# Windowed attention and a two-layer MLP on one core: chunk 0 in two halves, signs by the leaky function, words in pairs, two convolutions shared with VectorE

## The chip, the cores and the metric

One core of a Trainium2 chip runs the program. The time is device microseconds (us) from launch to end of one execution; the figure of a kernel is the median of its runs.

## What is computed

```python
# x (4, 4096, 192) and weight_gen (4, 4096, 8, 7) float32; w_in (192, 2048) and w_out (2048, 192) float64
w = softmax(weight_gen, axis=-1)                 # 7 taps for each of 8 heads of each token
out[b, s] = sum over k of w[b, s, :, k] * x[b, s - 6 + k]     # a causal convolution, 24 channels a head
h = out.reshape(16384, 192) @ w_in               # 16384 x 2048
g = maximum(0.01 * h, h)
y = g @ w_out                                    # 16384 x 192, float32
```

The two matrices come as 64-bit numbers, so a kernel reads them as pairs of 32-bit words and makes float32 values of them on the chip.

## The kernel before

**Tiling.** Partition p holds 128 consecutive tokens, its rows. A chunk is 4 rows of all partitions, that is 512 tokens; there are 32 chunks, and two chunks share one piece of loaded rows and softmax weights. The 2048 hidden units are 16 blocks of 128, taken two at a time in 8 steps per chunk (`NQ`).

**Work of a chunk.** GpSimd (POOL in the profile) convolves it (`conv_ops`: seven products of 768 elements per partition, six additions). The result is brought into the transposed form `xx`. TensorE multiplies with `w_in` (`mm1`), ScalarE (ACT) applies the leaky maximum, ScalarE and VectorE (DVE) split the result into a rounded part `gh` and a rest `gl`, and TensorE multiplies both with `w_out` into `po`. Operands of chunks 1 to 31 are split so, into two parts of a type that TensorE takes in one pass; a float32 product takes it four.

**Preparing the matrices.** Each of the 16 keys (8 steps, in and out) goes through stages: `read_words` (`r`, two ScalarE instructions, into `rnd` and `mag`), `widen` (`w` or `W`: VectorE shifts `mag` left by three, L121, then takes the sign in with a second instruction, L124), the rounding (`W`: VectorE L130; `o`: GpSimd L135), and, for later chunks, `upper_half` (`u` ScalarE L153, `U` VectorE L151) and `lower_half` (`L` VectorE, `l` GpSimd, L157). `spares` is a bank of PSUM that VectorE uses as scratch.

**The start.** Chunk 0 runs with the unsplit float32 values as they become ready (`mm1` with `value(...)`, `mm2_whole`, L437), so that the split parts are only wanted from chunk 1 on. Its convolution is divided by heads between VectorE (`d`, 20 of 32 row-heads, its products and its scratch in PSUM) and GpSimd (`g`). Chunk 1 is convolved by GpSimd alone (`p`), and so is chunk 2 (`q`, `feed`). `heat` issues 12 matmuls of zeros ahead of the first transposes. Chunks 0 and 1 are transposed by TensorE (`transposes`, L290; rows L299 and L300 move the result), later ones by VectorE and DMA.

**What sets the order.** Each engine runs its instructions in the order of the program. The string `START` lists the work of the start letter by letter: `s` is the next step of TensorE, the other letters are the stages above. Behind the string, `step` lays out the steady state.

## Time and profile before

| | |
|---|---|
| median of 3 runs | 1160.31 us (1159.36 to 1160.99) |
| the profiled execution's own time | 1161.17 us |
| its span, first to last instruction | 1159.4 us |
| TensorE busy | 1142.1 us (99%) |
| GpSimd, ScalarE, VectorE busy | 782.2, 645.1 and 514.2 us |
| mean granted TensorE clock | 0.998 |
| HBM read and written | 31.98 and 12.58 MB |

The span is what the rows of the trace add up to; the execution's own time is 1.8 us longer and holds what lies around it. The chain of waits is followed back from the last instruction and tells on which engine the end hangs at each moment. Busy shares are averages over the whole span: VectorE with 44% over all is busy 36.5 of the 40 us from 10 to 50, in the start.

### The profile page before, as it was taken

The page shows a single profiled execution, that of the slowest core. Times are in us where ns is not written, and L with a number is a line of the kernel's source. Part 1 is how long each engine was busy: PE and PEld are TensorE (multiplying, and loading weights), DVE is VectorE, ACT ScalarE, POOL GpSimd, SP SyncE. Part 2 cuts the span into 40 slices and gives each one's busy share as a digit, 9 for nine tenths or more (in the row PEclk, how much of TensorE's full clock was granted, in tenths as well). Part 3 has the DMA queues.
Part 4 walks back from the last instruction along what each step waited for, and adds up shares of the span by engine and source line. Part 5 has one row for each costly group of instructions (what it writes and reads, how often), then busy time and mean ns, then how long its engine had stood idle before and what let it go on. Part 6 is the DMA issues. An engine that isn't in the chain of part 4 may idle for free.

```text
span 1159.4 us, 30227 instructions
## 1 busy us (share of the span) xinstructions
PE 1142.1 (99%) x12660; PEld 1023.7 (88%) x12660; DVE 514.2 (44%) x829; ACT 645.1 (56%) x1173; POOL 782.2 (67%) x495
## 2 busy tenths in 40 slices
PE   5999999999999999999999999999999999999998
PEld 3689999999999999999999999999999999999997
DVE  7954343444334444344443444443444443444432
ACT  4656555565555555555555455555555555555554
POOL 7888687666687666787666786666786667876300
PEclk9999999999999999999999999999999999999999
DMA  8502422323233231322313224232322314222210
GB/s 230 156 18 73 119 55 70 115 53 99 67 91 92 56 104 49 111 70 70 108 48 109 56 69 120 51 103 60 110 72 60 108 43 121 60 69 56 52 46 15
DMA packets 43093, 93.70 MB, mean 81 GB/s; under 512 B 9679, under 2 KB 25167, under 8 KB 41166
## 3 DMA queue, kind: packets, MB, share of 16 engines
q1 hardware_dynamic: 42814, 91.59, 28.9%
q8 instruction: 99, 1.62, 0.6%
q14 instruction: 36, 0.29, 0.1%
q10 hardware_dynamic: 144, 0.20, 0.0%
HBM read 31.98 MB, written 12.58 MB: 38 GB/s over the span
## 4 chain that ended last, share of the span: by engine, by line
PE 98%; DVE 1%; DMA 0%; ACT 0%; issue 0%; SPq 0%; DVEq 0%
PE po L398 48%; PE hp L350 47%; PE po L437 2%; DMA xt<-in_x_dram 0%; DVE spares L251 0%; DVE acc L256 0%; PE ta L290 0%; DVE twice L266 0%; ACT hp L356 0%; DVE gl L373 0%; DVE xx L300 0%; ACT gh L372 0%; ACT xx L299 0%; DVE ot L474 0%; DVE bits L124 0%
## 5 line engine op out<-in xcount | busy, mean ns | idle before, releaser
L373 DVE TENSOR_TENSOR gl<-hp,gh 128x512 fp32r<-128x512 f32 x496 | 343.3, 692 | 558.1 <-ACT gh L372 557.5
L398 PE MATMUL po<-wo,gh 64*128 64x384 f32 x3968 | 581.3, 353 | 0.0
L356 ACT ACTIVATE hp<-hp 128x512 f32<-128x512 f32 x496 | 292.3, 589 | 434.3 <-PE hp L350 434.2
L398 PE MATMUL po<-wo,gl 64*128 64x192 f32 x3968 | 497.8, 248 | 0.3 <-DVE gl L373 0.3
L350 PE MATMUL hp<-xx,wi_h 64*128 64x512 f32 x2976 | 472.8, 395 | 0.1
L398 PEld LDWEIGHTS po<-wo,gl 64*128 64x128 f32 x3968 | 378.4, 187 | 11.1 <-DVE gl L373 0.5
L398 PEld LDWEIGHTS po<-wo,gh 64*128 64x128 f32 x3968 | 372.7, 184 | 11.8
L256 POOL TENSOR_TENSOR acc<-acc,tmp 128x768 f32<-128x768 f32 (+1 forms) x190 | 346.1, 1822 | 14.6
L372 ACT CAST gh<-hp 128x512 fp32r<-128x512 f32 x496 | 291.8, 588 | 38.6 <-PE po L398 24.8
L350 PEld LDWEIGHTS hp<-xx,wi_h 64*128 64x128 f32 x2976 | 260.2, 184 | 46.3 <-DVE xx L300 0.4
L251 POOL TENSOR_TENSOR tmp<-xt,wt 128x768 f32<-128x768 f32 (+1 forms) x192 | 291.8, 1520 | 12.4
L350 PE MATMUL hp<-xx,wi_l 64*128 64x512 f32 x1488 | 294.3, 391 | 0.0
L350 PEld LDWEIGHTS hp<-xx,wi_l 64*128 64x128 f32 x1488 | 140.1, 184 | 33.0
L310 POOL TENSOR_TENSOR split<-acc,split 128x768 fp32r<-128x768 f32 x30 | 55.3, 1843 | 167.4 <-ACT split L306 167.4
L474 DVE TENSOR_TENSOR ot<-po,ot 128x384 f32<-128x384 f32 x62 | 34.6, 558 | 69.6 <-ACT ot L473 69.2
L211 POOL TENSOR_TENSOR wt<-wt,mx 128x448 f32<-128x448 f32 (+1 forms) x16 | 15.2, 950 | 71.5 <-DVE mx L208 71.4
L319 DVE STREAM_TRANSPOSE sq<-split 128x384 f32<-128x384 f32 x120 | 58.5, 544 | 0.0
L251 POOL TENSOR_TENSOR acc<-xt,wt 128x768 f32<-128x768 f32 (+1 forms) x32 | 48.9, 1527 | 0.2
L225 POOL TENSOR_TENSOR wt<-wt,sm 128x448 f32<-128x448 f32 (+2 forms) x17 | 15.5, 915 | 37.6 <-DVE sm L222 29.5
L473 ACT COPY ot<-po 128x384 f32<-128x384 f32 x62 | 29.7, 479 | 6.4 <-PE po L398 3.6
L306 ACT CAST split<-acc 128x768 fp32r<-128x768 f32 x30 | 25.0, 833 | 0.0
L437 PEld LDWEIGHTS po<-bits,g 128*128 128x128 f32 x128 | 20.6, 190 | 4.9 <-DVE spares L121 1.5
(56 smaller groups left out, 219.6 us busy)
## 6 DMA issues: line engine op xcount, KB each, us to landing
xx<-sq SPq DMA_DIRECT2D x480, 96.0 KB, 2.2
xt<-in_x_dram SPq DMA_DIRECT2D x14, 1344.0 KB, 5.8
out_dram<-ot SPq DMA_DIRECT2D x63, 192.0 KB, 1.9
...
```

The lines of the kernel that those rows point to most:

```text
L251: ins = eng.tensor_tensor(out=out, in0=xv[:, s, :], in1=wk, op=ALU.mult).ins
L256: eng.tensor_tensor(out=acc[:, s, :], in0=acc[:, s, :], in1=out, op=ALU.add)
L310: eng.tensor_tensor(out=l, in0=att.pop(c), in1=h.bitcast(F32), op=ALU.subtract)
L319: nc.vector.transpose(out=sq[c][:, v, i], in_=src[:, v])
L350: nc.tensor.matmul(out=hp[2 * q + u], lhsT=w[s], rhs=r[s], start=(m == 0), stop=(m == len(passes) - 1),)
L356: return nc.scalar.activation(out=hp[n], in_=hp[n], func=AF.Prelu, alpha=0.01).ins
L372: nc.scalar.copy(out=h, in_=t)
L373: nc.vector.tensor_tensor(out=l, in0=t, in1=h.bitcast(F32), op=ALU.subtract)
L398: ins = nc.tensor.matmul(out=po[j // HALF][:, j % HALF, 0:d], lhsT=g[n][s, j * P:(j + 1) * P], rhs=wo[s, f, 0:d], start=(f == 0 and i < HA ...
L437: nc.tensor.matmul(out=po0[:, j // 2, j % 2 * D:(j % 2 + 1) * D], lhsT=g_h[n][:, j * P:(j + 1) * P], rhs=value((n // 2, OUT))[:, n % 2], s ...
L473: nc.scalar.copy(out=ot, in_=po[k][:, :, D:2 * D])
L474: nc.vector.tensor_tensor(out=ot, in0=po[k][:, :, 0:D], in1=ot, op=ALU.add)
```

## The change

Six things are changed, all in the first 90 us of the program.

- Chunk 0 is computed in two halves of two rows (`first_step`, 16 steps of 256 tokens). The first half runs in float32 as before. The second half takes the split parts of `w_in` and of its tokens (`split_passes`), so `wi_h` and `wi_l` are wanted eight steps earlier. Both halves still multiply with the unsplit `w_out` values. Only the first two rows are convolved ahead of the first transposes (`d` and `g`, 10 of 16 row-heads on VectorE); the other two are GpSimd's alone (`e`).
- ScalarE's leaky function with a slope of -2^32 makes `mag`, so that its bits carry the sign; VectorE's second instruction of `widen` (L124) is gone.
- Words come in pairs of blocks: runs of 2048 and 3072 bytes instead of 1024 and 1536, in half as many issues. Hidden units are dealt to the blocks in another order, the same for both matrices.
- VectorE convolves one of four rows of chunk 1 (`P`) and two of four rows of chunk 2 (`Q`), with its scratch `tmpd` in SBUF.
- `heat` is three portions of 5 instead of one of 12.
- The order `START` is new. More of the casts (`U`) are VectorE's: 10 instead of 1.

```diff
 START = (
-    "ASdrrggggdgddggdggadgdrwgZdgddddgdobTWrppppppppWpkKWrspWrrWsrrsWWMrpspWr"
-    "WruspLrUuWrLWuEsDrwrLsouWWuLLuqqWlqquqsqLLqquqqqIusLLusuqsLuLquCVyuqqLsL"
-    "YLusXqqqXqqsqqXqlXqsqs"
+    "ArSdZggdggddddggggdgZgddZgaddgdgrjdbTreesUjjUKrjerrwsjLpurseoeleeerrjjre"
+    "seursWuejrersepjrjjrpUpjlLrsstppUUUjplLPpPsulsUpPpppPPsssspMLkLPEUPPPPDl"
+    "PuPqPlQlUqsQsQqQqqIqqUsqqQQqsqlQlQqqQQQqqsQQCVsuyYslqXqqXqqqqsqXXqslqqqs"
+    "q"
 )


...
+    def load_words(j, kind):
+
         if kind == IN:
-            w = raw.tile([P, NB, P, 2], U32, tag="wi", name="wi_raw", bufs=3)
+            w = raw.tile([P, NB, 2 * P, 2], U32, tag="wi", name="wi_raw", bufs=2)
             for u, r in enumerate(HALVES):
-                f = 2 * q + u
-                eng.dma_start(out=w[r], in_=w_in_words[:, :, f * P:(f + 1) * P, :])
+                f = u * DFF // 2 + 2 * j * P
+                nc.sync.dma_start(out=w[r], in_=w_in_words[:, :, f:f + 2 * P, :])
+            w = w.rearrange("p b (m v) w -> p v b m w", v=2)
         else:
-            w = raw.tile([P, 2, D, 2], U32, tag="wo", name="wo_raw")
-            eng.dma_start(out=w, in_=w_out_words[:, 2 * q:2 * q + 2, :, :])
-        words[key] = w
+            w = xtp.tile([P, 2, 2, D, 2], U32, tag="xx", name="wo_raw", bufs=2)
+            nc.sync.dma_start(out=w, in_=w_out_words[:, :, j])
+            w = w.rearrange("p u v d w -> p v u d w")
+        for v in range(2):
+            words[2 * j + v, kind] = w[:, v]

     NW = NB * P
     vals = {}

...
-        nc.scalar.activation(out=rnd, in_=w[:, :, 0], func=AF.Copy, scale=2.0 ** -29)
-        nc.scalar.activation(out=mag, in_=w[:, :, 1].bitcast(F32), func=AF.Copy, scale=REBIAS)
+        w = words.pop(key)
+        rnd = raw.tile([P, NW], U32, tag="rnd", name="rnd", bufs=4)
+        mag = raw.tile([P, NW], F32, tag="mag", name="mag", bufs=4)
+        a = NB if key[1] == IN else 2
+        flat = [t.rearrange("p (a b) -> p a b", a=a) for t in (rnd, mag)]
+        nc.scalar.activation(out=flat[0], in_=w[..., 0], func=AF.Copy, scale=2.0 ** -29)
+        nc.scalar.activation(
+            out=flat[1], in_=w[..., 1].bitcast(F32), func=AF.Prelu, scale=REBIAS, alpha=SIGN
+        )
         vals[key] = rnd, mag.bitcast(U32)

...
+    def widen(keys, add=False):
+
+        slots = [spare().bitcast(U32) if add else None for _ in keys]
+        for key, t in zip(keys, slots):
+            rnd, mag = vals[key]
+            bits = raw.tile([P, NW], U32, tag="bits", name="bits", bufs=NV)
+            vals[key] = bits, rnd
+            if t is None:
+                t = bits
+            nc.vector.tensor_scalar(
+                out=t, in0=mag, scalar1=3, scalar2=None, op0=ALU.logical_shift_left
+            )
+        for key, t in zip(keys, slots):
+            if add:
+                bits, rnd = vals[key]
+                nc.vector.tensor_tensor(out=bits, in0=t, in1=rnd, op=ALU.add)
+                vals[key] = bits.bitcast(F32)

...
+    def conv_ops(c, eng, tag, r0=0, n=J, inner=None, outer=None, tmp=None, w=None):

         if c not in att:
             att[c] = conv.tile([P, J, D], F32, tag="acc", name="acc", bufs=2)
-        acc = att[c].rearrange("p r (h g) -> p (r h) g", g=G)
-        q, i0 = c // 2, c % 2 * J
+        acc = att[c][:, r0:r0 + n, :].rearrange("p r (h g) -> p (r h) g", g=G)
...
             s = inner if k else outer
-            n = s.stop - s.start
-            xv = xt[q][:, i0 + k:i0 + k + J, :].rearrange("p r (h g) -> p (r h) g", g=G)
-            wk = w[:, s, k:k + 1].to_broadcast([P, n, G])
+            m = s.stop - s.start
+            xv = xt[q][:, i0 + k:i0 + k + n, :].rearrange("p r (h g) -> p (r h) g", g=G)
+            wk = w[:, s, k:k + 1].to_broadcast([P, m, G])
             if k == K - 1:
                 out = acc[:, s, :]
             else:
-                t = conv.tile([P, J * D], F32, tag=tag, name=tag) if tmp is None else tmp
-                out = t[:, 0:n * G].rearrange("p (h g) -> p h g", g=G)
+                if tmp is None:
+                    t = conv.tile([P, n * D], F32, tag=tag, name=tag)
+                else:
+                    t = tmp[:, k % 2 * TOK:(k % 2 + 1) * TOK]
...
+    def transposes_first(h):
+
+        if h:
+            new_xx(0)
+        for b in range(NB):
+            t = ps_h.tile([P, TOK], F32, tag="h", name="ta")
+            for j in range(HALF):
+                v = twice[0][:, (h * HALF + j) * NB + b].rearrange("p u d -> p (u d)")
+                nc.tensor.transpose(out=t[:, j * P:(j + 1) * P], in_=v, identity=ident)
+            if h == 0:
+                if b == 1:
+                    nc.vector.tensor_copy(xx0[:, b], t[:, 0:HT])
+                else:
+                    nc.scalar.copy(out=xx0[:, b], in_=t[:, 0:HT])
+                continue
+            t = t[:, 0:HT].rearrange("p (j t) -> p j t", j=HALF)
+            hi, lo = (xx[0][:, 0:HALF, v, b, :] for v in range(2))
+            nc.scalar.copy(out=hi, in_=t)
+            nc.vector.tensor_tensor(out=lo, in0=t, in1=hi.bitcast(F32), op=ALU.subtract)
...
+    def split_passes(i, tokens):
+
+        assert (i, IN) in halved
         passes = []
         for b in range(NB):
-            h, l = xx[c][:, :, 0, b, :], xx[c][:, :, 1, b, :]
-            w_h, w_l = wi_h[:, i, b, :], wi_l[:, i, b, :]
-            if c == 0:
-                passes.append((value((i, IN))[:, b], h))
-            else:
-                passes += [(w_h, h), (w_h, l), (w_l, h)]
+            (h, l), w_h, w_l = tokens(b), wi_h[:, i, b, :], wi_l[:, i, b, :]
+            passes += [(w_h, h), (w_h, l), (w_l, h)]
+        return passes
+
...
+    def first_step(m):
+
+        h, i = divmod(m, NQ)
+        if h == 0:
+            passes = [(value((i, IN))[:, b], xx0[:, b]) for b in range(NB)]
+        else:
+            passes = split_passes(
+                i, lambda b: [xx[0][:, 0:HALF, v, b, :] for v in range(2)]
+            )
+        hs = [ps_h.tile([P, TOK], F32, tag="h", name="hp")[:, 0:HT] for u in range(2)]
+        products(passes, hs)
+        for u in range(2):
+            g = gp.tile([P, TOK], F32, tag="gh", name="g")[:, 0:HT]
+            nc.scalar.activation(out=g, in_=hs[u], func=AF.Prelu, alpha=0.01)
+            g_h[2 * m + u] = g
+        if m >= 2:
+            mm2_whole(m - 2)

...
+    def mm2_whole(m):
+
+        h, i = divmod(m, NQ)
+        for u in range(2):
+            for j in range(HALF):
                 nc.tensor.matmul(
-                    out=po0[:, j // 2, j % 2 * D:(j % 2 + 1) * D],
-                    lhsT=g_h[n][:, j * P:(j + 1) * P], rhs=value((n // 2, OUT))[:, n % 2],
-                    start=(n == 0 and j % 2 == 0), stop=(n == NF - 1 and j % 2 == 1),
+                    out=po0[:, h, j * D:(j + 1) * D],
+                    lhsT=g_h[2 * m + u][:, j * P:(j + 1) * P], rhs=value((i, OUT))[:, u],
+                    start=(i == 0 and u == 0 and j == 0),
+                    stop=(i == NQ - 1 and u == 1 and j == HALF - 1),
                     skip_group_check=True,
...
-    stages = dict(r=read_words, w=widen, o=round_up, u=upper_half, l=lower_half)
-
-    stages["W"] = lambda key: widen(key, True)
+    stages = dict(r=read_words, o=round_up, u=upper_half, l=lower_half)
...
-        w0 = po0[:, 0, 0:J * HK].rearrange("p (h k) -> p h k", k=K)
+        w0 = po0[:, 0, 0:HALF * HK].rearrange("p (h k) -> p h k", k=K)
         away = spares.rearrange("p a b -> p (a b)")
+        parts = slice(0, G0), slice(0, (HALF - C0) * H)
+        rest = slice(G0, HALF * H), slice((HALF - C0) * H, HALF * H)
         conv0 = dict(
-            d=conv_ops(0, nc.vector, None, slice(0, G0), slice(0, (J - C0) * H), away, w0),
-            g=conv_ops(0, nc.gpsimd, "tmp", slice(G0, J * H), slice((J - C0) * H, J * H)),
-            p=conv_ops(1, nc.gpsimd, "tmp"),
+            d=conv_ops(0, nc.vector, None, 0, HALF, *parts, away, w0),
+            g=conv_ops(0, nc.gpsimd, "tmp", 0, HALF, *rest),
+            e=conv_ops(0, nc.gpsimd, "tmp", HALF, HALF),
+            P=conv_ops(1, nc.vector, "tmpd", 0, C1),
+            p=conv_ops(1, nc.gpsimd, "tmp", C1, J - C1),
+            Q=conv_ops(2, nc.vector, "tmpd", 0, C2),
         )
+
...
             elif what == "A":
                 tell(softmax_max(0, FIRST))
-                load_words(order[0])
+                load_words(0, IN)
                 load_weights(0, SECOND)
-                load_words(order[1])
-                load_rows(0, ((PAD + J, PAD + R),))
-                load_words(order[2])
-                load_words(order[3])
+                load_rows(0, ((PAD + HALF, PAD + R),))
+                load_words(1, IN)
+                load_words(0, OUT)
                 softmax_sub(0, nc.vector, FIRST)
                 softmax_exp(0, FIRST)
             elif what == "S":
```

TensorE at its start. The names: `ta<-ident,twice` are the transposes, `hp` the first product, `po` the second. Before:

```order
L290 MATMUL ta<-ident,twice 128x128 x12
L350 MATMUL hp<-xx,bits 128x512 x18
L437 MATMUL po_105<-bits,g 128x192 x8
L350 MATMUL hp<-xx,bits 128x512 x6
L437 MATMUL po_105<-bits,g 128x192 x8
```

Now:

```order
L330 MATMUL ta<-ident,twice 128x128 x6
L394 MATMUL hp<-xx0_89,bits 128x256 x18
L509 MATMUL po_106<-bits,g 128x192 x4
L394 MATMUL hp<-xx0_89,bits 128x256 x6
L509 MATMUL po_106<-bits,g 128x192 x4
```

Half as many transposes and second products, and first products of half as many columns, stand in each step; there are twice as many steps.

VectorE between the last words and the transposed chunk 1 (`xx<-ta,xx` is its lower half, which TensorE waits for). Before:

```order
L130 ISA bits<-spares,rnd 128x768
L157 TENSOR_TENSOR wo<-bits,wo 128x2x192
L157 TENSOR_TENSOR wi_l<-bits,wi_h 128x384
L121 TENSOR_SCALAR spares<-mag 128x384
L124 SCALAR_TENSOR_TENSOR spares<-mag,spares 128x384
L130 ISA bits<-spares,rnd 128x768
L157 TENSOR_TENSOR wi_l<-bits,wi_h 128x384
L157 TENSOR_TENSOR wo<-bits,wo 128x2x192
L300 TENSOR_TENSOR xx<-ta,xx 128x4x128 x3
```

Now, from the lower half of chunk 0's second rows to the last words and the first products of chunk 1:

```order
L340 TENSOR_TENSOR xx<-ta,xx 128x2x128 x3
L172 CAST wi_h<-bits 128x384 x2
L172 CAST wo<-bits 128x2x192
L143 TENSOR_SCALAR spares<-mag 128x384
L149 ISA bits<-spares,rnd 128x768
L178 TENSOR_TENSOR wi_l<-bits,wi_h 128x384
L283 TENSOR_TENSOR acc<-xt,wt 128x192
L283 TENSOR_TENSOR tmpd<-xt,wt 128x192
L172 CAST wo<-bits 128x2x192
L280 TENSOR_TENSOR acc<-acc,tmpd 128x192
```

and from the end of VectorE's row of chunk 1 to the lower half of the transposed chunk 1:

```order
L283 TENSOR_TENSOR tmpd<-xt,wt 128x192
L306 TENSOR_TENSOR twice<-acc,tmpd 128x3x64
L283 TENSOR_TENSOR acc<-xt,wt 128x384
L172 CAST wo<-bits 128x2x192
L283 TENSOR_TENSOR tmpd<-xt,wt 128x384
L280 TENSOR_TENSOR acc<-acc,tmpd 128x384
L283 TENSOR_TENSOR tmpd<-xt,wt 128x384
L355 TENSOR_TENSOR xx<-ta,xx 128x4x128 x3
```

Three casts stand ahead of the last words, and five instructions of chunk 2 and of the casts stand between `twice`, which the transposes of chunk 1 read, and the lower half of their result.

## Rows read from the trace of the kernel before

**Rows 1.** The page, part 4: the chain that ended last, share by engine.
```profile
PE 98%; DVE 1%; DMA 0%; ACT 0%; issue 0%; SPq 0%; DVEq 0%
```

**Rows 2.** The chain of waits in order of time: start us, us, what.
```profile
17.19 2.80 PE ta L290 x12
...
28.26 2.80 PE po L437 x16
31.06 2.78 PE hp L350 x12
...
60.76 2.35 PE hp L350 x16
63.11 5.40 PE po L437 x32
68.51 4.38 PE hp L350 x36
72.89 2.27 PE po L398 x32
```

**Rows 3.** Timeline, TensorE, second set of transposes: start us, us, engine, line, operation.
```profile
58.76 1.47 PE L290 MATMUL ta<-ident,twice 128*128 128x128 f32 x12
```

**Rows 4.** Windows of 1 us, TensorE: busy, granted clock (PEclk), DMA share, GB/s.
```profile
16.00:17.00 1.00, 0.00 (x0) 1.00 1.12 300
...
18.00:19.00 1.00, 1.00 (x7) 0.50 0.15 28
```

**Rows 5.** Timeline, VectorE and GpSimd, convolution of chunk 0.
```profile
5.62 0.65 DVE L251 TENSOR_TENSOR acc<-xt,po 128x480 f32<-128x480 f32 x1
...
6.19 0.69 POOL L251 TENSOR_TENSOR acc<-xt,wt 128x288 f32<-128x288 f32 x1
...
7.61 0.79 POOL L256 TENSOR_TENSOR acc<-acc,tmp 128x288 f32<-128x288 f32 x1
...
13.30 0.58 POOL L211 TENSOR_TENSOR wt<-wt,mx 128x224 f32<-128x224 f32 x1
...
15.50 0.52 POOL L251 TENSOR_TENSOR tmp<-xt,wt 128x192 f32<-128x192 f32 x1
...
16.10 1.14 POOL L266 TENSOR_TENSOR twice<-acc,tmp 128x192 f32<-128x192 f32 x2
```

**Rows 6.** Timeline, VectorE, casts and differences with both inputs in SBUF.
```profile
37.80 1.96 DVE L151 CAST wi_h<-bits 128x384 fp32r<-128x384 f32 x1
...
52.27 0.55 DVE L157 TENSOR_TENSOR wi_l<-bits,wi_h 128x384 fp32r<-128x384 f32 x1
...
54.49 1.37 DVE L157 TENSOR_TENSOR wi_l<-bits,wi_h 128x384 fp32r<-128x384 f32 x1
55.78 1.90 DVE L157 TENSOR_TENSOR wo<-bits,wo 128x384 fp32r<-128x384 f32 x1
```

**Rows 7.** Timeline, GpSimd, at the same times.
```profile
37.43 2.11 POOL L256 TENSOR_TENSOR acc<-acc,tmp 128x768 f32<-128x768 f32 x1
...
52.56 1.11 POOL L157 TENSOR_TENSOR wo<-bits,wo 128x384 fp32r<-128x384 f32 x1 [0.64 <-ACT wo L153]
53.63 1.81 POOL L256 TENSOR_TENSOR acc<-acc,tmp 128x768 f32<-128x768 f32 x1
55.52 1.74 POOL L251 TENSOR_TENSOR tmp<-xt,wt 128x768 f32<-128x768 f32 x1
57.34 2.02 POOL L256 TENSOR_TENSOR acc<-acc,tmp 128x768 f32<-128x768 f32 x1
59.44 1.54 POOL L251 TENSOR_TENSOR tmp<-xt,wt 128x768 f32<-128x768 f32 x1
```

**Rows 8.** Groups of instructions from 0 to 60 us: busy us, mean ns, idle before.
```profile
L124 DVE SCALAR_TENSOR_TENSOR spares<-mag,spares 128x384 uint32<-128x384 uint32 x14 | 7.9, 561 | 0.5
L130 DVE CUSTOM_DVE_ANT_0 bits<-spares,rnd 128x768 uint16<-128x768 uint16 x14 | 7.8, 557 | 0.8
...
L112 ACT ACTIVATE rnd<-wi_raw 128x384 uint32<-128x384 uint32 x8 | 4.5, 560 | 8.3 <-DMA wi_raw<-in_moe_w_in_dram 8.0 <-ACT mag L113 0.2
```

191 lines of the change are left out of this document (97 added, 94 removed).

## The prediction

> **What bounds the kernel now.** The first view to read is the chain that ended last: TensorE holds 98% of it [rows 1]. A change can therefore gain only where TensorE gets less to do, starts earlier, or stands still less. The chain in order of time says where that could be [rows 2]. TensorE's first useful work, the transposes of chunk 0, begins at 17.19 us; from then to 63.11 it goes through chunk 0 and the first product of chunk 1, each step of chunk 0 costing 2.78 for the first product (12 float32 passes) and 2.80 for the second. At 63.11 two leftover second products of chunk 0 follow (5.40), and at 68.51 the split steady state begins. The change leaves what comes from there to 1159.4 as it is, so I compare the moment that answers to 68.51.
>
> Two further views belong to it. The windows show that TensorE's granted clock was at its lower level (0.50, 1.2 GHz) while the first transposes ran, after a window in which TensorE did nothing [rows 4]; those 12 took 2.80, the next 12 took 1.47 at full clock [rows 3]. And the timelines of VectorE and GpSimd side by side show what no busy share shows: a VectorE instruction with both inputs in SBUF does not run beside a GpSimd instruction. The one at 52.27 started while GpSimd was idle and took 0.55. The one at 54.49 took 1.37: GpSimd's instruction ended at 53.63 + 1.81 = 55.44, VectorE's 0.42 later. The next started at 55.78 and took 1.90, again 0.42 behind GpSimd's end at 57.26; and a cast, started at 37.80, ended 0.22 behind GpSimd's [rows 6, 7]. These waits cost nothing before, since few of them stood in front of anything that TensorE wanted.
>
> **The change part by part.** All is counted against the profiled span, 1159.4; its execution took 1161.17, 0.86 above the median of 1160.31, and I add the difference to the median.
>
> *Earlier start.* Half the rows are convolved before the first transposes. GpSimd's share is the later one. Its costs per element follow from the rows: products 0.52 at 192 and 0.69 at 288 elements, additions 0.79 at 288 and 1.81 at 768, the softmax subtraction 0.58 at 224 [rows 5, 7]. That gives 0.44 for a product and 0.48 for an addition of 144, 0.77 for the subtraction of 336, 1.00 for the last addition of 384. Six products of 144, one of 192, five additions, the subtraction and the last addition are 2.64 + 0.52 + 2.40 + 0.77 + 1.00 = 7.33; some 11 gaps of 0.08 (0.79 + 0.08 is the usual distance) make 8.2. It begins about 0.3 earlier than 6.19, as the first softmax has half the elements. 5.9 + 8.2 = 14.1: **3.1 earlier**. VectorE's share (0.65 at 480 elements, so about 0.41 at 240) is done a microsecond before that.
>
> *TensorE's work.* First half of chunk 0: eight first products on half the columns, between 1.39 (half of 2.78) and 1.51 (if 0.07 per pair of passes is fixed), I take 1.45; six second products on half the rows, 1.40 each: 11.6 + 8.4 = 20.0. Second half: the first product is 18 single-pass matmuls in 9 pairs. Pairs of 512 columns cost 4.38 / 18 = 0.243, pairs of 288 on average 2.27 / 16 = 0.142 [rows 2], so 256 columns cost 0.13 and the step 1.16; with eight second products 9.3 + 11.2 = 20.5. The last two second products, 2.8, come behind chunk 1's first product. Transposes: 0.73 + 0.73 + 1.47; chunk 1's first product 2.19. Sum 48.4. Three times TensorE waits for the transposed tile to be moved: 4.35 - 1.47 - 2.19 = 0.7 for chunk 1 (58.76 to 63.11), some 0.4 for each half-size one: 1.5. Before, the stretch from 17.19 to 68.51 was 51.3, now 49.9: **1.4 less**, of which 1.3 is the clock. If the clock is low under the first six transposes they cost up to 0.7 more; portions of `heat` now come up to their start, so I take none. Without further waits the kernel gains 4.5: 1155.8.
>
> *Signs.* Fourteen of the sixteen removed L124 took 7.9 us of VectorE [rows 8]. VectorE was not on the path; ScalarE's instruction for `mag` keeps its size. Nothing by itself. *Words in pairs.* ScalarE waited 8.0 us for words of `w_in` [rows 8], TensorE never did. The bytes are the same, the runs twice as long: between 0 and, if two large buffers come free later than three small ones, the same 0 as long as ScalarE keeps ahead (a rival below).
>
> *VectorE's share of chunks 1 and 2, and nine more casts.* This is the part that adds waits. VectorE's own work is small: 192 elements with both inputs in SBUF cost 0.35 alone (0.55 at 384). But `tmpd`, `xt`, `wt` and the casts' sides are all SBUF, and GpSimd is convolving at the same time, with instructions of 576 elements, 1.20 and 1.40 long by the prices above. By rows 6 and 7 each such VectorE instruction ends 0.2 to 0.4 after the end of the GpSimd instruction that it meets, and the next one meets the next: one VectorE instruction per GpSimd instruction, 1.3 to 1.5 us instead of 0.35. I walk through VectorE's order behind the lower half of chunk 0's second rows, which is done near 38.0 (14.1 + 0.7 + 0.4 + 20.0 = 35.2, with about 0.8 of waits for the first words 36.0; transposes and the moving add 2.0).
>
> - Three casts stand ahead of the last words. At 1.35 each they end at 42.1; shift and rounding (0.56 + 0.56) give the words at 43.2. TensorE wants them after 36.0 + 1.1 + 1.16 + 1.40 + 1.16 = 40.9. **Wait 2.3** (0 if the casts meet an idle GpSimd: 38.0 + 1.05 + 1.1 = 40.2).
> - Seven more at 1.3 take VectorE to 52.2, where GpSimd's part of chunk 1 is done and it waits for VectorE's maximum for the next softmax. Then VectorE is nearly alone: maximum 0.6, two differences 1.7 (one meets the subtraction), six short products, additions and a cast 2.0, the sums 1.35, one more 0.35, together 6.0, to 58.2; the last two of chunk 1 meet GpSimd again, 1.0 each, to 60.2; ScalarE's copy of 768 elements, some 0.8, gives 61.0. TensorE wants chunk 1 at 43.2 + 1.40 + 6 x 2.56 = 60.0. **Wait 1.0.**
> - The transposes end at 62.5. Their lower half stands behind five instructions of chunk 2 and casts, 1.1 each: 60.2 + 5.5 + 0.7 = 66.4, where 62.8 would do. **Wait 3.6.** This is the largest.
> - Behind it VectorE has nine more instructions of chunk 2, 0.55 alone and up to 1.8 each, among the differences `gl` of chunk 1, which TensorE waits for. **Wait 1.0 to 1.7**, I take 1.5.
>
> The sum is 2.3 + 1.0 + 3.6 + 1.5 = 8.4 of new waits against 4.5 gained: 3.9 longer, or 1160.3 + 3.9 = **1164.2**. The weakest term is the meeting of the two engines: VectorE's instructions are short, so 2% on GpSimd's durations moves each wait by up to one GpSimd instruction.
>
> A rule goes further here. The rows show a GpSimd instruction behind such a meeting lengthened by 0.20 to 0.29 (1.74 against 1.54, 2.02 against 1.81, 2.11 against 1.81) [rows 7]. The Trainium skill, SBUF — State Buffer, section Who interferes with whom, says that whoever has the shared port pair holds it for the whole instruction and the other fully blocks; by that rule GpSimd would lose VectorE's 0.55. The waiting agrees with the trace; the length does not, as VectorE's start-up falls into its wait, and I price it by the rows.
>
> **The rivals.**
>
> *VectorE's waits are hidden (faster).* The place is the same: from 38 to 66 us. If VectorE's instructions mostly fall into GpSimd's gaps, or the last words and `xx` come in time, TensorE goes through as in the sum without waits: 1155.8. For it: GpSimd is idle in places, and VectorE's own work from 38 to the lower half of chunk 1 is only some 14 us of 22. It decides when fewer than about six of the 26 such instructions in that stretch wait. Against it: all three that met GpSimd in rows 6 waited to its end.
>
> *Half of it hidden (no change).* The casts and `twice` come in time, the five of chunk 2 do not: -4.5 + 3.6 + 1.0 = about 1160.4. The point is whether GpSimd's durations of 576 elements are a few per cent shorter than I interpolate.
>
> *GpSimd loses the whole instruction.* If its instructions lengthen by 0.41, VectorE's reading time, and not by 0.20, the ten waits in the first two places grow by 0.2 each: 2 us, 1166.2. The sentence of the skill above would bring this about.
>
> *ScalarE paces the first half.* Each step now has four reads of words of 0.56 and two leaky functions of at most 0.56 in 2.85 us of TensorE: 3.36 if nothing overlaps [rows 8]. Up to 0.5 a step, 4 us: 1168.
>
> **How the numbers follow.** Forecast 1164.2 with chance 0.5, its own range 1162.7 to 1167.5; GpSimd loses more 0.07; ScalarE paces 0.05; half hidden 0.18; all hidden 0.2. Faster by over 0.2% (below 1158.0; that is about the least that a measurement of this kernel can tell from no change) is nine tenths of the hidden case with a fifth of the middle one: 0.22. Within 0.2%, up to 1162.6, is what is left of these two and the low end of the forecast: 0.19. Slower: 0.59. The range reaches up to 1168, where ScalarE paces, and down to 1156.5, which takes in about half of the hidden case.
>
> **What would show it.** In the changed profile the first transposes should start near 14 at full clock; the steps of the first half cost 2.85, those of the second 2.56. The casts L172 and the products L283 of VectorE with `tmpd` should have means of 1 us and more, ending 0.2 to 0.4 behind GpSimd's; the chain should name VectorE's `bits`, `twice` and `xx` between 38 and 66, some 7 us together. If L283 on VectorE has a mean near 0.4 instead, the sum falls back to 1156. If the first half's steps are 3.3 apart with ScalarE in the chain, the fourth rival holds. If the steady state behind it is not as long as before, my comparison at 68.51 was too short.

## The result and the profile after

The changed kernel takes 1172.9 us (median of 4 runs, 1172.68 to 1173.32), the kernel before 1160.3: a ratio of 1.011, interval 1.0092 to 1.0127. It is 12.6 us slower where 3.9 were predicted. Its profiled execution took 1172.68 with a span of 1170.6, 11.2 longer than that of before.

Before itself gives two times: of 19 executions in one batch, 11 took 1159.35 to 1159.79 at a mean granted clock of 0.999 to 1.000 and 8 took 1160.70 to 1161.01 at 0.998, and the profile behind [rows 2, 4] is of the second kind (1161.17).

Below, "before" and "after" are the two kernels. The page of after, chain by engine, answers to [rows 1]: TensorE's share of the chain fell from 98% to 91%.

```profile
PE 91%; DVE 4%; ACT 2%; issue 1%; SPq 1%; DMA 1%; ACTq 0%
```

The chain of after in order of time (start us, us, what) answers to [rows 2].

```profile
13.72 1.47 PE ta L330 x6
15.19 2.67 PE hp L394 x12
...
20.18 0.78 ACT mag L129
21.74 0.66 ACT g L428 x2
22.80 0.79 ACT rnd L128
...
41.42 1.77 DVE wi_h L172 x2
43.20 1.07 DVE wo L172
...
67.76 0.69 DVE xx L355
68.49 3.91 PE hp L394 x17
72.40 2.80 PE po L509 x16
75.20 2.34 PE hp L394 x18
...
84.25 1.80 DVE tmpd L283
86.07 1.78 DVE acc L280
87.85 1.20 DVE gl L446 x2
...
97.20 0.59 SPq L384
97.83 0.59 SPq L384
...
107.15 2.54 PE po L469 x32
```

From 18 to 36 the chain runs mostly through ScalarE, from there to 68 through VectorE, from 80 to 90 again, and from 97 to 107 through SP's queue, where the 16 transfers of chunk 2 are issued one by one (0.59 each), late. The point that answers to 68.51 of before is 75.20, 6.7 later; another 4.5 are lost behind it. What TensorE waited for behind 60 (us in total, times, longest):

```profile
PE hp L394 <- DVE xx L355: 3.0, 1, 3.0
PE po L469 <- DVE gl L446: 2.1, 1, 2.1
PE po L469 <- SPq L483: 0.6, 1, 0.6
```

Behind two of these waits the granted clock (PEclk, the third number from the right) goes to its lower level, 0.50, as it did under the first transposes of before [rows 4]. Windows of after:

```profile
68.00:69.00 1.00, 0.51 (x4) 0.42 (x6) 1.00 (x3) 0.00 (x0) 0.92 (x2) 0.81 0.00 0
70.00:71.00 1.00, 1.00 (x8) 0.81 (x6) 0.00 (x0) 0.00 (x0) 0.92 (x2) 0.50 0.00 0
...
91.00:92.00 1.00, 1.00 (x8) 0.80 (x6) 0.00 (x0) 0.97 (x3) 0.89 (x1) 0.50 0.00 0
```

The product at 68.49 took 3.91 (17 of its 18 records) where the same product of before took 2.35 at full clock (16 of 18) [rows 2].

The transfers are late because chunk 2 is. GpSimd's first product of it, before and after:

```profile
48.89 1.54 POOL L251 TENSOR_TENSOR acc<-xt,wt 128x768 f32<-128x768 f32 x1
```

```profile
61.68 0.99 POOL L283 TENSOR_TENSOR acc<-xt,wt 128x384 f32<-128x384 f32 x1
```

The last additions of chunk 2 after, GpSimd's for its two rows and VectorE's for the other two, and then ScalarE's rounding of the whole chunk in before (that of after, at 90.20, is shown further down):

```profile
82.59 1.21 POOL L292 TENSOR_TENSOR acc<-acc,tmp 128x384 f32<-128x384 f32 x1
89.55 0.56 DVE L292 TENSOR_TENSOR acc<-acc,tmpd 128x384 f32<-128x384 f32 x1
```

```profile
76.50 0.84 ACT L306 CAST split<-acc 128x768 fp32r<-128x768 f32 x1
```

GpSimd is done at 83.80, VectorE at 90.11: in the changed kernel the rounding waits for VectorE's rows.

### The profile page after: what moved, and what is told of

Its sections match the earlier page's. It is cut to its first block, busy times and chain, and to the rows that moved or that the text cites. A ratio compares the mean times of both kernels' runs of the same rounds, so it can differ in the third digit from the quotient of the medians.

```text
span 1170.6 us, 30566 instructions
## 1 busy us (share of the span) xinstructions
PE 1149.8 (98%) x12807; PEld 1035.5 (88%) x12807; DVE 525.5 (45%) x842; ACT 648.2 (55%) x1183; POOL 788.4 (67%) x515
## 4 chain that ended last, share of the span: by engine, by line
PE 91%; DVE 4%; ACT 2%; issue 1%; SPq 1%; DMA 1%; ACTq 0%
PE po L469 47%; PE hp L394 44%; DVE tmpd L283 1%; SPq L384 1%; DVE acc L280 1%; DMA wt<-in_weight_gen_dram 1%; ACT rnd L128 0%; ACT mag L129 0%; DVE wo L172 0%; ACT g L428 0%; ACT hp L434 0%; DVE gl L446 0%; PE po L509 0%; DVE spares L143 0%; DVE wi_l L178 0%
## 5 line engine op out<-in xcount | busy, mean ns | idle before, releaser
L394 PE MATMUL hp<-xx,wi_h 64*128 64x512 f32 (+1 forms) x3072 | 485.2, 393 | 4.1 <-DVE xx L355 3.0
L394 PEld LDWEIGHTS hp<-xx,wi_h 64*128 64x128 f32 x3072 | 269.2, 185 | 52.9 <-DVE xx L355 3.3
L394 PE MATMUL hp<-xx,wi_l 64*128 64x512 f32 (+1 forms) x1536 | 302.6, 389 | 0.0
L283 POOL TENSOR_TENSOR tmp<-xt,wt 128x768 f32<-128x768 f32 (+3 forms) x198 | 290.8, 1469 | 12.6
L280 POOL TENSOR_TENSOR acc<-acc,tmp 128x768 f32<-128x768 f32 (+3 forms) x165 | 288.3, 1747 | 12.5
L394 PEld LDWEIGHTS hp<-xx,wi_l 64*128 64x128 f32 x1536 | 145.9, 185 | 33.4
L292 POOL TENSOR_TENSOR acc<-acc,tmp 128x768 f32<-128x768 f32 (+1 forms) x30 | 54.7, 1823 | 2.4
L283 POOL TENSOR_TENSOR acc<-xt,wt 128x768 f32<-128x768 f32 (+3 forms) x33 | 48.7, 1477 | 0.2
```

Source lines behind the costliest of these rows:

```text
L280: eng.tensor_tensor(out=acc[:, inner, :], in0=acc[:, inner, :], in1=held, op=ALU.add)
L283: ins = eng.tensor_tensor(out=out, in0=xv[:, s, :], in1=wk, op=ALU.mult).ins
L292: eng.tensor_tensor(out=acc, in0=acc, in1=out, op=ALU.add)
L394: nc.tensor.matmul(out=out, lhsT=w[s], rhs=r[s], start=(m == 0), stop=(m == len(passes) - 1))
```

## Experiments

All times are medians; the kernel before in the same batches took 1159.7 to 1160.8. Gains are against the 1172.9 of after unless another run is named. The executions of one version spread by 0.3 to 3.9 us, most by 0.8 to 1.7, so a gain under 1 is hardly told from none.

### The clock under the first transposes, and the signs alone

```diff
-                heat(12)
+                heat(21)
```

> The kernel before with 21 instead of 12 matmuls of zeros ahead of the first transposes. The 12 end 2.10 us before the transposes begin at 17.19, and these run at the lower clock (2.80 instead of 1.47 at full clock). Nine more at 0.21 end near 17.0. If the clock there costs time, the transposes take 1.47 and the kernel 1158.9. If the first products wait for their words anyway, as the changed kernel's runs suggest (its second transposes began at 38.57 with the lower clock from 14.01 to 17.42 and at 38.58 in a run without it), the time stays at 1160.3.

Run e7: 1159.70, ratio 0.9998 (0.9988 to 1.0008). The ten executions lie between 1159.34 and 1160.66, seven of them within the first group of before or 0.01 below it and two at 1160.1; all ten have a mean granted clock of 0.999 or 1.000. So the slower group is all but gone, and the median does not move because that of before (1159.68 in this batch) was in the first group already.

```diff
-        nc.scalar.activation(out=mag, in_=w[:, :, 1].bitcast(F32), func=AF.Copy, scale=REBIAS)
+        nc.scalar.activation(out=mag, in_=w[:, :, 1].bitcast(F32), func=AF.Prelu, scale=REBIAS, alpha=SIGN)
...
-        nc.vector.scalar_tensor_tensor(
...
```

> The kernel before with one part of the change alone: ScalarE's leaky function carries the sign into mag, and VectorE's second instruction L124 is gone. 14 of these took 7.9 us of VectorE from 0 to 60. If nothing waits for VectorE in the kernel before, as the chain of waits says (TensorE holds 98% of it), the time stays at 1160.3. Rival: the words come earlier and TensorE's first products of chunk 0 with them: up to 0.5 less. Against that, if the leaky function reads slower than the copy, ScalarE's 16 instructions for mag get longer than 0.55 and TensorE waits.

Run e8: 1159.48, ratio 1.0000 (0.9991 to 1.0010): the signs are worth nothing by themselves. The timeline of its profiled execution shows the same transposes as those of before at full clock, 1.57 where [rows 2] has 2.80:

```profile
16.94 1.57 PE L288 MATMUL ta<-ident,twice 128*128 128x128 f32 x12 [1.02 <-DVE twice L264]
```

There the point of 68.51 lies at 66.70. In 11 of the 19 executions of before, this and not 68.51 is what the halves had to beat.

### The first half: reads and transfers

```diff
-            w = w.rearrange("p b (m v) w -> p v b m w", v=2)
+            w = w.rearrange("p b (v m) w -> p v b m w", v=2)
...
-        "(u j p v) (d w) -> p u j v d w", u=2, p=P, v=2, w=2
+        "(j u v p) (d w) -> p j u v d w", u=2, p=P, v=2, w=2
```

> In the changed kernel ScalarE's read of a block of w_in words takes 0.93 us (x16), that of w_out words 0.62, where both took 0.56 before. Theory: a block's words now lie 16 bytes apart in the fetched pair (the two blocks alternate), 8 before, and it is this that slows the read. Here the two blocks of a pair lie one behind the other, so a block's words are 8 bytes apart again; pairs, bytes and issues stay as they are, only the w_out words come in runs of 1536 bytes instead of 3072. By the theory the 16 reads fall to about 0.56, ScalarE leaves the chain between 18 and 36 us, TensorE's gaps of 0.50, 0.18 and 0.86 in the first half close and the second transposes begin near 37.0 instead of 38.57. If TensorE's lateness there is handed on to the end, the kernel takes 1171.4; if VectorE and GpSimd set what comes behind it, it stays at 1172.9. Rival: the reads are slow because of the leaky function or of transfers that land beside them; then they stay at 0.93 and nothing moves.

Run e1: 1172.21. Groups on ScalarE (busy us, mean ns | idle before), after:

```profile
L128 ACT ACTIVATE rnd<-wi_raw 128x384 uint32<-128x384 uint32 x8 | 7.5, 934 | 6.3 <-DMA wi_raw<-in_moe_w_in_dram 6.3
...
L128 ACT ACTIVATE rnd<-wo_raw 128x384 uint32<-128x384 uint32 x8 | 5.0, 621 | 0.0
```

and in this run:

```profile
L128 ACT ACTIVATE rnd<-wo_raw 128x384 uint32<-128x384 uint32 x8 | 4.4, 549 | 1.8 <-DMA wo_raw<-in_moe_w_out_dram 1.8
L128 ACT ACTIVATE rnd<-wi_raw 128x384 uint32<-128x384 uint32 x8 | 4.4, 547 | 7.4 <-DMA wi_raw<-in_moe_w_in_dram 7.4
```

The spacing explains the reads: 934 ns at 16 bytes, 547 at 8. The Trainium skill, SBUF — State Buffer, section Specifications (TRN2), has the rule that would have told it: lines of 16 bytes, each of which must be hit twice for full bandwidth. But the second transposes stayed (38.68 for 38.57): the place of the reads is taken by the transfer of the `w_out` words (one piece of this run's chain: `21.92 10.02 DMA wo_raw<-in_moe_w_out_dram`). So I took most of that transfer away:

```diff
+            if not kept:
+                kept.append(xtp.tile([P, 2, 2, D, 2], U32, tag="xx", name="wo_raw", bufs=2))
+                nc.sync.dma_start(out=kept[0], in_=w_out_words[:, j])
+            w = kept[0]
```

> The run on reads with three of the four fetches of w_out words left out (2.3 of 6.3 MB of words; the first pair's words are used in their place, so the products with w_out are not those of the reference); every read, shift, cast and matmul stays. With the reads at 0.55 us the chain of waits held 10 us of the transfer of w_out words between 22 and 32 us, and TensorE waited 1.30 at 34.3. Theory: in the first half all words must be fetched in some 24 us and the transfers set its pace; without a third of them the second transposes begin near 37.2 instead of 38.7, and VectorE's chain behind them comes as much earlier to the end, 1170.7 instead of 1172.2. Rival: ScalarE's and VectorE's work on each key sets the pace whatever lands; then the second transposes stay at 38.7.

Run e6: the second transposes begin at 37.54, 1.1 earlier, as the theory had it. But the time is 1172.09 where the theory had 1170.7: TensorE then waits 1.32 for the last words and 3.66 for `xx`. What VectorE and GpSimd do behind the second transposes sets the end.

### The wait for xx, and the clock behind it

```diff
-    "PuPqPlQlUqsQsQqQqqIqqU..."
+    "PuPqPllqssqqqIQUQQQqqU..."
```

> The five VectorE instructions (four of chunk 2's convolution and a cast) that stand ahead of the lower half of the transposed chunk 1 are put behind it; nothing else moves. Theory: they cause TensorE's wait of 3.02 at 65.47, and the wait causes the half clock from 68.62 to 72.04, under which the first product of chunk 1 takes 3.91 instead of about 2.1. Both go: the wait falls to 0.7, the product to 2.1, and the second products that begin at 72.33 begin near 68.2, so 4.1 earlier: 1168.8 if it is kept to the end. Rival: VectorE has the same work to do while GpSimd is convolving, so the five only move, and the differences of chunk 1 (the gap of 2.07 at 86.4) or the transfers of chunk 2 (0.57 at 106.6) get later by as much; then the point at 72.33 moves but the time stays within 1 us of 1172.9.

Run e2: 1170.38, 2.5 gained, where 4.1 were forecast. The point at 75.20 moves to 71.07, by 4.1 as forecast; the rest is given back behind it, in other waits:

```profile
PE po L469 <- DVE gl L446: 1.4, 3, 0.9
PE po L469 <- SPq L483: 1.3, 1, 1.3
PE hp L394 <- DVE gl L446: 1.2, 1, 1.2
```

In this run the first half was at full clock, and its second transposes still began 24.8 behind the first, as in after (13.72 to 38.57): the lower clock at the start costs nothing, the words are waited for.

```diff
                 transposes(1)
+                fill = ps_h.tile([P, TOK], F32, tag="h", name="fill")
+                for _ in range(14):
+                    nc.tensor.matmul(
+                        out=fill, lhsT=zeros[:, 0:P], rhs=zeros, start=True, stop=True
+                    )
```

> Fourteen matmuls of zeros (128 x 512) are put between the transposes of chunk 1 and its first product, so that TensorE works through the wait at 65.47 to 68.49; nothing else moves. It measures the clock by itself. If the half clock from 68.62 on follows from the wait, the granted clock stays at full speed, the first product of chunk 1 takes about 2.1 instead of 3.91, and the kernel gains up to 1.8, 1171.1; the gaps of 2.07 and 0.57 behind it stay. If what comes behind is set by VectorE and GpSimd anyway, the gap at 86.4 grows by what is gained and the time stays at 1172.9. If the clock falls whatever TensorE does there, the product stays at 3.9.

Run e3: 1171.55 (1170.22 to 1172.32), 1.4 gained. The clock stays at 1.00 and the point at 75.20 moves to 74.30: half of the 1.7 only, since the product, begun at 68.53, is now held up to 69.13 by the next piece of `xx`.

### VectorE beside GpSimd

```diff
         for k in reversed(range(K)):
+            if lean and 0 < k < K - 1:
+                yield
+                yield
+                continue
...
-            p=conv_ops(1, nc.gpsimd, "tmp", C1, J - C1),
+            p=conv_ops(1, nc.gpsimd, "tmp", C1, J - C1, lean=True),
```

> The changed kernel with ten of GpSimd's thirteen instructions for chunk 1 left out (its products and additions of the five middle taps; three of four rows of chunk 1 are therefore not those of the reference). VectorE's instructions and their order stay. It measures the meeting of the two engines. Theory: VectorE's instructions with both inputs in SBUF are long only because each waits to the end of a GpSimd instruction, so from 41 to 54 us, where GpSimd now has next to nothing, the casts and products of 0.86 to 1.58 fall to 0.34 to 0.55: 13 of them, some 9 us; the last words come 3 us earlier and TensorE's wait of 0.50 for them goes, VectorE is done with its share of chunk 1 well before TensorE asks for it, and with GpSimd early as well the wait of 3.02 before the first product of chunk 1 shrinks below 1.5. Rival: the instructions take that long by themselves (VectorE's reading of SBUF beside ScalarE and TensorE); then they stay above 1 us and nothing on VectorE moves.

Run e9: 1169.77 (1168.37 to 1172.25). Timeline of after, first VectorE, then GpSimd:

```profile
46.79 1.58 DVE L283 TENSOR_TENSOR tmpd<-xt,wt 128x192 f32<-128x192 f32 x1
48.30 1.36 DVE L172 CAST wo<-bits 128x384 fp32r<-128x384 f32 x1
49.58 1.58 DVE L280 TENSOR_TENSOR acc<-acc,tmpd 128x192 f32<-128x192 f32 x1
```

```profile
46.62 1.54 POOL L280 TENSOR_TENSOR acc<-acc,tmp 128x576 f32<-128x576 f32 x1
48.24 1.21 POOL L283 TENSOR_TENSOR tmp<-xt,wt 128x576 f32<-128x576 f32 x1
49.52 1.42 POOL L280 TENSOR_TENSOR acc<-acc,tmp 128x576 f32<-128x576 f32 x1
```

Each VectorE instruction ends 0.21 or 0.22 behind a GpSimd one (48.37 behind 48.16, 49.66 behind 49.45, 51.16 behind 50.94). The same three in this run, with nothing on GpSimd from 45.47 to 47.88:

```profile
45.61 0.34 DVE L287 TENSOR_TENSOR tmpd<-xt,wt 128x192 f32<-128x192 f32 x1
45.88 0.35 DVE L172 CAST wo<-bits 128x384 fp32r<-128x384 f32 x1
46.14 0.34 DVE L284 TENSOR_TENSOR acc<-acc,tmpd 128x192 f32<-128x192 f32 x1
```

1.58, 1.36 and 1.58 fall to 0.34 and 0.35: that VectorE waits for GpSimd's instructions is shown. TensorE's wait for the last words goes with it. The wait for `xx` does not (2.67; I had below 1.5): the five instructions ahead of it meet GpSimd's chunk 2 instead. Nor does every instruction of VectorE's share wait: of the thirteen of `P` in after, seven took 1.05 to 1.58 and six, where GpSimd was idle, 0.29 to 0.36.

```diff
-    "...rrsstppUUUjplLPpPsulsUpPp..."
+    "...rrsstppuuujplLPpPsulsupPp..."
```

> Three edits of the changed kernel together: words of a pair one block behind the other (as in the run on reads), the five VectorE instructions behind the lower half of chunk 1 (as in the run that puts xx first), and, new, the last seven of VectorE's ten casts given to ScalarE, which is busy 8.86 of the 25 us from 38 to 63 in the changed kernel while VectorE is busy 24.62. Theory: VectorE is what sets the pace from 38 to 94 (the chain of waits names it there almost without a break), so its seven casts, 6.8 us as they meet GpSimd's instructions, come off the chain: the last words come about 3 us earlier and TensorE's wait of 0.50 for them goes, the waits behind the transposes of chunk 1, 4.5 in all with the xx put first, fall below 1.5: 1166.5 to 1167.5. Rival: GpSimd sets the pace and VectorE only waits for it; then the casts' time is filled with longer meetings, the waits stay near 4.5 and the time is 1170, as with the xx first alone.

Run e5 (four of the seven casts are in the lines above): 1167.15, 5.8 gained in all; 3.2 of it is more than with the xx first alone, and the reads gave 0.7 by themselves, so the casts are worth some 2.5 if the gains add up: VectorE paced the stretch. Behind 70, TensorE still waits 2.4 (I had below 1.5), for `gl` and for ScalarE.

### Who convolves chunk 2

```diff
-C2 = 2
+C2 = 0
...
-            Q=conv_ops(2, nc.vector, "tmpd", 0, C2),
```

> VectorE's two rows of chunk 2 are given back to GpSimd, which convolves all four; the order of all other work stays. Theory that VectorE's share costs more than it gives: four of the five instructions ahead of the lower half of chunk 1 go (the wait of 3.02 falls to about 1, the half clock behind it goes: 3.8), and so does the gap of 2.07 at 86.4 with the half clock behind it (1.7 more): the kernel is near 1166. Rival: GpSimd needs the help: 14 instructions grow from some 1.0 to 1.5 and 1.85 us, 9 us in all, chunk 2 is convolved near 97 instead of 90, its 16 transfers of some 10 us land near 111, TensorE wants it near 100 and waits some 10 us in one place; the time stays near 1172 to 1176.

Run e4: 1172.01 (1171.29 to 1173.00), 0.9 gained, hardly more than nothing. The time is the rival's, the way is not: chunk 2's rounding starts at 90.15, not near 97. That is the moment of after (90.20), where VectorE's two rows came last; now GpSimd's four do, at 90.11, and what is saved on VectorE is lost in one wait of 5.1, to 92.23, for ScalarE, which waited 11.60 in this rounding.

```diff
-C1 = 1
+C1 = 0
...
-            P=conv_ops(1, nc.vector, "tmpd", 0, C1),
...
-    "...PPsssspMLkLPEUPPPPDlPuPqPl..."
+    "...ppsssspMLkLEuDluql..."
```

> Halves, signs and pairs without VectorE's share: on top of the run with the casts (words one behind the other, the last seven casts ScalarE's), VectorE convolves no row of chunk 1 or 2, GpSimd all of them. GpSimd's 13 instructions of chunk 1 grow from some 1.2 and 1.4 to 1.54 and 1.81, less what it no longer loses to VectorE: chunk 1 is convolved near 57 instead of 53.7, which is before TensorE asks for it (63.0 in the run with the casts): no wait there, the point at 70.18 stays. Chunk 2 is then convolved near 88 to 90, and TensorE waits behind it: 5.1 in one place in the run without VectorE's share of chunk 2. Theory (GpSimd is short of time because the second half of chunk 0 and nine lower halves are its own now): 1168 to 1171. Rival (the shares cost more than they give): no wait over 2 us behind 70 and 1164 to 1165.

Run e10: 1173.28 (the run without `Q` and the casts on ScalarE are in it too), slower than either theory: GpSimd is later than I thought, chunk 2 done at 91.2, and TensorE waits in one place for ScalarE, which waits for it. Against e5, from which it differs by the shares, it is 6.1 slower: there VectorE's shares give more than they cost.

```profile
PE po L468 <- ACT gh L444: 7.4, 1, 7.4
```

```diff
-    "...jplLpsulsuppppsssspMLkLEuDluqllqssqqq..."
+    "...jpLLpsuLsuppppsssspMLkLEuDLuqLLqssqqq..."
```

> As the run without shares, and the eight lower halves that GpSimd still has behind the second transposes are VectorE's, as most of them were before. That takes some 8 to 9 us off GpSimd: chunk 1 is convolved near 54, chunk 2 near 81 to 82, the 16 transfers end near 97 and TensorE is not kept waiting behind 70. If so the end is 1163 (70.2 for the point that was 66.7 to 68.5 before, and the rest as before), which is what the halves cost with the sharing undone: the second transposes at 39.5 instead of 37.2 without waits, and steps of 3.00 and 2.75 instead of 2.85 and 2.56. Rival: if chunk 0 in halves by itself is worth what was predicted for it without waits, 1156 to 1158.

Run e11: 1167.14. Neither 1163 nor 1157: chunk 2 is convolved at 85.5, not 82. ScalarE's rounding of chunk 2, after and in this run (in brackets the idle time ahead of it and what ended it):

```profile
90.20 0.83 ACT L361 CAST split<-acc 128x768 fp32r<-128x768 f32 x1 [8.15 <-DVE acc L292]
```

```profile
85.56 0.83 ACT L360 CAST split<-acc 128x768 fp32r<-128x768 f32 x1 [9.58 <-POOL acc L291]
```

The leaky functions of the next step are queued behind the waiting instruction. I put it one step later:

```diff
-    "...qqqqsCVsuyYs..."
+    "...qqqqssCVuyYs..."
```

> The run without shares whose lower halves are VectorE's, and ScalarE's instruction that rounds the convolved chunk 2 (with GpSimd's difference behind it) stands one step of TensorE later. In that run ScalarE waited 9.58 us in this instruction for GpSimd's last addition of chunk 2 (to 85.56), with the leaky functions of the next step queued behind it, and TensorE stood still for 2.98 at 84.56 and ran 90.4 to 93.5 at the lower clock. Theory: GpSimd's end at 85.5 itself is early enough, the wait came only from what is queued behind the waiting instruction; one step later TensorE is busy to 88.9 and nothing waits: 3.5 of waits and 1.0 to 1.4 of clock go, 1162.5 to 1163.5, and what is left against the kernel before (1159.4 to 1161.2) is TensorE's work and start alone. Rival: the 16 transfers of chunk 2 (11 us behind 91) are the next to be late: TensorE wants them near 104 and they land there; then up to 2 us are given back, 1164 to 1165.

Run e12: 1167.27, nothing gained on e11. This execution reached the point of 69.13 only at 72.11 (its words came later, second transposes at 39.58 against 37.90), so that the wait of 2.98 is gone says little about the queue. What it does show is the rival: the transfers of chunk 2, from 91.79, are the next to be late, and TensorE, 3.0 later at the point than in e11, ends only 0.5 later.

```profile
91.79 10.80 SPq L383 DMA_DIRECT2D xx<-sq  x16
```

TensorE waits 1.9 for instructions of SP that stand behind them.

### GpSimd's time, and chunk 2 by itself

| | chunk 2's rounding starts | time |
|---|---|---|
| before (three kernels) | 74.7 to 76.5 | 1159.5 to 1160.3 |
| six extra products on GpSimd | 81.0 | 1164.5 |
| lean second half (two runs) | 82.1, 82.4 | 1164.1, 1164.3 |
| lower halves on VectorE; casts on ScalarE; later rounding | 85.6 to 86.3 | 1167.1 to 1167.3 |
| xx first | 88.3 | 1170.4 |
| after, fill, reads, no `w_out`, no `Q` | 89.3 to 90.2 | 1171.6 to 1172.9 |
| no shares | 91.2 | 1173.3 |

The moments are those of the profiled executions. Over these versions the time follows this moment (the run with chunk 1 lean, 86.4 and 1169.8, lies off the line). "Lean" here means that the products and additions of the five middle taps are left out. Five runs ask whether it is the cause. The first three: GpSimd's `e` of chunk 0 lean (second diff below); the same with the `w_out` fetches left out; and before with more for GpSimd (first diff):

```diff
-    "...obTWrppppppppWpkKW..."
+    "...obTWrzzzzzzppppppppWpkKW..."
...
+            elif what == "z":
+                nc.gpsimd.tensor_tensor(out=extra, in0=extra, in1=extra, op=ALU.mult)
```

```diff
-            e=conv_ops(0, nc.gpsimd, "tmp", HALF, HALF),
+            e=conv_ops(0, nc.gpsimd, "tmp", HALF, HALF, lean=True),
```

> The version without shares and with VectorE's lower halves (1167.1), and ten of GpSimd's thirteen instructions for the second half of chunk 0 left out (its middle taps; two of four rows of chunk 0 are not those of the reference): some 10 us less for GpSimd, 0.86 and 1.00 each with their gaps. Theory: it is GpSimd's ten us more in chunk 0 that the start lacks; chunk 2 is convolved near 76 instead of 85.5, TensorE's wait of 2.98 and the lower clock behind it go, and the kernel takes 1162 to 1163. What is then left against the kernel before is TensorE's own. Rival: what came later with GpSimd only hid another lateness (the transfers of chunk 2, VectorE's lower halves); then a wait of 2 us or more stands in its place and the time stays above 1165.

Run e13: 1164.29, 2.9 gained on e11, less than thought. Chunk 2 comes only 3.2 earlier, since its softmax weights wait for an exponential of ScalarE that stands behind the leaky functions of a step of TensorE (54.6). TensorE's steps are bare here (chain; the first two rows are the first half, the others the second):

```profile
34.59 1.50 PE hp L397 x12
36.09 1.50 PE po L512 x8
...
40.10 1.50 PE po L512 x8
41.60 1.26 PE hp L397 x18
```

> As the run with the lean second half, and three of the four fetches of w_out words left out as well (the first pair's words in their place). Theory: the second transposes come 1 to 1.5 earlier than there (37.5 with these fetches left out before, 37.9 to 39.6 with them), and now nothing behind them is set by VectorE or GpSimd, so that it is kept to the end: 1160.5 to 1161.5. That is the halves with nearly all waits taken away; the prediction had 1155.8 for them. Rival: the end stays where it was, as it did when the fetches were left out of the changed kernel itself.

Run e14: 1164.05, the rival. The second transposes came only 0.2 earlier.

> The kernel before with six products of 768 elements (1.54 us each, some 9.6 with their gaps) added on GpSimd ahead of the convolution of chunk 1, on a tile that nothing else reads. Nothing else is changed. Theory: GpSimd's end of chunk 2 decides; there it ends at 75.9, and with the idle 3.6 at 43 used up it would end near 82. ScalarE's rounding of chunk 2 waits for it with the leaky functions queued behind it, TensorE stands still about 2 us near 82 and runs a few us at the lower clock: 1162 to 1163.5. Rival: the kernel before has the slack (chunk 2 is wanted only near 102 us), and the time stays at 1159.4 to 1161.

Run e15: 1164.46, 3.6 more than before: the start has no ten us of GpSimd to give. But the place is not the one I named. Chunk 2, at 81.0, was in time; TensorE waited for last words that GpSimd rounds, and for `xx`:

```profile
PE hp L350 <- POOL bits L135: 1.7, 1, 1.7
PE hp L350 <- DVE xx L300: 1.5, 1, 1.5
```

The last two runs take away the middle taps of chunk 2 alone, from the version without shares and from the changed kernel itself (there on `Q` as well).

```diff
-                    convs.append([last + 1, conv_ops(last + 1, nc.gpsimd, "tmp", r0, J - r0)])
+                    convs.append([last + 1, conv_ops(last + 1, nc.gpsimd, "tmp", r0, J - r0, lean=last == 1)])
```

> The version without shares and with VectorE's lower halves (1167.1), with ten of GpSimd's thirteen instructions of chunk 2 left out (its middle taps; chunk 2 is not that of the reference). Up to the first product of chunk 1 nothing is changed. Theory: the moment at which chunk 2 is ready decides; ScalarE's rounding of it starts near 76 instead of 85.6, TensorE's waits of 2.98, 0.28 and 0.27 and the lower clock behind them go, 4.5 in all: 1162.5, and what is left is the point at 69.1 against 66.7 to 68.5. Rival: both are late from the same thing (words, VectorE) and the waits stay: 1166 to 1167.

Run e16: 1162.56, 4.6 gained on e11, as forecast to 0.1. Its rounding of chunk 2 does not wait, and TensorE's waits of 2.98, 0.28 and 0.27 are gone:

```profile
76.19 0.84 ACT L364 CAST split<-acc 128x768 fp32r<-128x768 f32 x1
```

With chunk 2 as early as in before it is still slower than before, by a ratio of 1.0017 (1.0007 to 1.0027): the rest has other causes.

> The changed kernel with the middle taps of chunk 2 left out on both engines (ten of VectorE's instructions, ten of GpSimd's; chunk 2 is not that of the reference). Theory: three of the five VectorE instructions ahead of the lower half of chunk 1 go (TensorE's wait of 3.02 falls below 1.5 and the product behind it from 3.91 to about 2.2), the gap of 2.07 for gl with its lower clock and the 0.57 of SP's queue go as well: 3.3 before 75 and 4.3 behind, 1165 to 1166; the rest against the kernel before is the first half and the steps. Rival: what is taken out here is filled by the next lateness, and no more than 3 is gained: 1170.

Run e17: 1164.33, under the 1165 to 1166 of the theory; 8.6 of the 12.6 us are gone. The executions took 1164.11, 1164.26, 1164.41 and 1167.64. The profiled one is the last: its words came late and its second transposes only at 43.23, but it has neither the wait for `xx` nor that for `gl`, and behind the point it needs 1091.2, where before needs 1090.9 and after 1095.4. That is shown: two thirds of the loss is chunk 2's convolution, which comes too late for what is queued behind it and holds VectorE when TensorE wants `xx` and `gl`. The run does not part VectorE's share of this from GpSimd's. The last third is read from the chain below and not tested by itself.

None of these versions beats the kernel before; those with the signs or the longer `heat` alone are level with it.

## Why the prediction was wrong, step by step

Two steps failed, the comparison at 68.51 and the gain of 4.5 without further waits; the lower clock had no term.

- **The comparison at 68.51** is the first: the change "leaves what comes from there to 1159.4 as it is". The prediction named its own test (too short if the steady state behind it is not as long), and that is what happened: 4.5 behind the point, where the walk had 1.5. They are 2.07 of waiting for `gl`, 0.57 for SP's queue and some 1.7 of lower clock from 89; 0.2 is left. The walk followed VectorE to the lower half of `xx` and to `gl` and took GpSimd only as the partner that VectorE meets; no term asked when chunk 2 is done. In before its rounding starts at 76.50, in after at 90.20. GpSimd has the second half of chunk 0 to itself now and starts chunk 1 in earnest at 33.6 instead of 19.4, and chunk 2 at 61.68 instead of 48.89. `P` and `Q` were to carry that. But they wait where GpSimd works (e9), and `Q` ends 6.3 behind GpSimd's own rows; without `Q` chunk 2 is ready at the same moment (e4), without `P` and `Q` a little later (e10).
- **Earlier start**: right in time, 13.72 for 14.1, but not at full clock as the prediction expected. What it gains goes into waits for words in the first half (e1, e2, e6), where fourteen of the sixteen keys are now wanted in 25 us, and into TensorE's longer work.
- **TensorE's work**, and with it the gain of 4.5, was mis-sized by 2.8. A step of the first half costs 3.00 (I had 2.85), of the second 2.75 (2.56). The fixed part could be read in [rows 2]: 32 second products 5.40, 16 of them 2.80, so 0.1625 each and 0.20 a group, and 8 cost 1.50, not half of 2.80. And "1.3 is the clock" was a gain over one execution only; the kernel before has it in 11 of 19. From its first transposes at full clock (16.94) to the point at 66.70 before needs 49.8; the halves, without the two waits for words in e13, 52.9 from 13.69. So the halves without these waits are worth 3.2 less 3.1, about nothing, where I had 4.5: the rival with the waits hidden would have been level, not faster. e16, in which chunk 2 is in time but words are still waited for, takes 1162.6.
- **Words in pairs, 0**: wrong in ScalarE's reads (0.93 for 0.56). The rival in which ScalarE paces the first half (chance 0.05) was right in its place, gaps of 0.50, 0.18 and 0.86; curing the reads gained 0.7 at most, since the transfers came next.
- **Signs, 0**: right, on the kernel before (e8).
- **VectorE's meetings**: the mechanism was right, the places were sized unevenly. Predicted 2.3, 1.0, 3.6 and 1.5; measured 0.50 for the last words, 0.03 for chunk 1, 2.3 for `xx` above its normal 0.7, and 2.07 for `gl`. The first two were small because TensorE came late too: it wanted the last words at 44.9, not 40.9. That these waits were put too long is luck for the forecast: it hid 4.1 of what was missing elsewhere.
- **The rule weighed** (the Trainium skill, SBUF — State Buffer, section Who interferes with whom): that the other is blocked for the whole instruction holds for VectorE's waiting (e9). GpSimd's additions of 576 took 1.41 to 1.54 in after and its products 1.21 to 1.40: it loses 0 to 0.2, not VectorE's whole instruction. The pricing by rows stands.
- **The clock in the new waits** had no term. It shows as 1.7 under the product at 68.49, about as much from 89, and as 1.1 over the first transposes and the product behind them; the fill gave 0.9 back at the point for the first.

Ledger against the prediction, in TensorE's time, from the starts of its pieces in after: start -0.4; steps +2.8; lower clock at the start +1.1 and first-half gaps +1.5 (one replaces the other, as e2 shows); second transposes and the moving of their result +1.1; the three waits 2.8 instead of 6.9, -4.1; the product behind the wait for `xx` +2.1, 1.7 of it the lower clock; behind the point +3.0: 7.1 of the 7.3 by which the span exceeds the forecast one. The other 1.4 of the miss lies outside the span: the sum was set against a profiled execution 0.86 above its median, and that of after is 0.2 below its own, with 2.1 outside its span where before had 1.8.
